# Router logits of 18 tiles summed on VectorE, keys turned once per block, a GpSimd drain per expert unit, and a new order of the first loads

## The chip, the core and the metric

The kernel runs on one core of one Trainium2 chip. The metric is the device time of one execution in microseconds (us), and the time of a version is the median of its runs. The core has TensorE (PE, matmuls; PEld is its weight load), VectorE (DVE), ScalarE (ACT), GpSimd (POOL) and SyncE (SP, which here only issues transfers).

## What is computed

Local attention, a dense MLP and a mixture of experts with one expert per token, one behind the other, over 3072 tokens of 512 features:

```python
# attention: batch 4, heads 8, seq 768, head_dim 64; chunks of 32 queries see
# 8 memory keys, 16 keys to the left, their own 32, and 8 to the right
scores = scale * (q_c @ k_full.T); a = exp(scores - max); a /= sum(a) + 1e-9
out[chunk] = a @ v_full
# MLP, 512 -> 2048 -> 512
h = x @ w_in; g = h * tanh(softplus(h)); y = g @ w_out
# experts: 8, 512 -> 1024 -> 512
xn = y / (norm(y) + 1e-6); en = expert_emb / (norm(expert_emb) + 1e-6)
logits = xn @ en.T / tau; e = argmax(logits); gate = softmax(logits)[e]
out = gate * (relu(y @ w1[e]) @ w2[e])
```

All matmuls that matter are done with operands split into a high and a low float32r part, three products each.

## The kernel before, in words

**The work and its tiles.** 24 attention pairs (128 queries of all heads each) fill 8 blocks of 384 tokens. The MLP goes through 128 units: a unit is one block with one slice of 128 of the 2048 hidden features, 12 matmuls into `p_h` (`mm_h`), the activation on ACT and DVE, 9 matmuls into `p_y` (`mm_y`). Blocks 0 and 1 do their first 8 slices, then block 2 all 16, then blocks 1 and 0 their second 8, then the others. A block yields three tiles of 128 tokens: 24 tiles. Behind the MLP come 16 expert units of one or two slots of 128 gathered tokens.

**What sets the order.** Everything is written down as jobs in a `Plan`: a key, a function, the engines that may do it with a cost, a rank, what it comes after, and which buffers it gets or uses. `Plan.order` picks at each step the job of lowest rank that can start by the planner's own costs and latencies, and by that fixes the order on every engine and on each queue. `NUDGE` is a table of offsets to the ranks. Engines run their queue in order. Until the first `mm_h`, wherever the planner sees PE waiting, it puts in *fills*: matmuls on constants (`p_fill`, L1573) whose result nobody reads.

**Keys, per pair** (`pairs`, L420). Three transposes on PE: the queries (`p_qT`, 128 columns), one key tile of 104 rows (`p_kT`: memory keys and the front of the window) and a second one of 72 rows (`p_k`), with their own loads `load_k1` and `load_k2`; five copies `kT(m)` (L517) spread them into the four windows of 64 keys that the scores use. Neighbouring windows overlap, so some keys are loaded and turned twice.

**Weights of the MLP** (`piece`, L351). 32 pieces of 512 KB, loaded by SP (L360, L363), each then taken apart on DVE with ACT and POOL beside it: sign, bias, high, low, and the parts `hi` and `lo`. The first blocks wait for these pieces.

**Rows of a finished tile** (`rows`, L796). The tile is scaled (`out`), stored to `y_d`, turned on PE (`T`, L832, `p_yT`, 4 transposes), split into three bf16 parts (`b1` a cast on ACT or DVE, `r1` L844, `b2`, `b3` L850) and multiplied with the bf16 parts of the expert embedding in 12 matmuls (`L`, L864, `p_lg`), which DVE adds up (`L2`, L870). The last three tiles (`i >= T1`) take a float32 form instead: a copy and 4 float32 matmuls (L859). ACT squares the row and sums it (`sq`, L853).

**Expert units** (`unit`, L1257). Gathers and scatters of rows are indirect transfers that POOL issues (L1278, L1500); POOL also makes three of the eight low weight parts per unit (L1356). Behind the scatters of units 5, 10 and 14 stands a `drain` of POOL (`RETIRE`, L1593).

## Time and profile before

| | |
|---|---|
| median of 3 runs (lowest, highest) | 1026.44 us (1025.91, 1028.74) |
| the profiled execution, its own time | 1026.37 us |
| span of that execution | 1024.6 us |
| PE busy | 1000.1 us, 98% |
| DVE busy | 756.4 us, 74% |
| ACT busy | 670.8 us, 65% |
| POOL busy | 184.8 us, 18% |
| moved by DMA | 129.06 MB, mean 126 GB/s |
| mean granted TensorE clock | 0.995 |

The span runs from the first to the last instruction that the profile holds, and the execution's own time is 1.8 us longer. "Busy" is the time in which an engine had at least one instruction in work. PE at 98% over the whole says little by itself: matmuls overlap and fills count as busy. What bounds the kernel has to be read stage by stage.

### The profile page before, as it was taken

What the parts mean: (1) busy time and instruction counts of PE and PEld (TensorE: products, weight loads), DVE (VectorE), ACT (ScalarE), POOL (GpSimd) and SP (SyncE); (2) the same over time, 40 slices, a digit from 0 to 9 for tenths busy, and PEclk for the clock granted to TensorE, in tenths of its full rate; (3) what the DMA queues carried; (4) which work ended last, traced back from release to release, by engine and by line L of the source; (5) the groups of instructions that cost most, each with busy time, mean ns of one, the idle gap of its engine ahead of it and who ended that gap; (6) DMA issues with size and microseconds to landing.
All of it is one profiled execution on the core that took longest, in us unless ns stands there. A gap on an engine that the chain in (4) does not pass through costs nothing. (4 is left out here: it accounts for less than half of the span.)

```text
span 1024.6 us, 23081 instructions
## 1 busy us (share of the span) xinstructions
PE 1000.1 (98%) x8875; PEld 886.0 (86%) x8875; DVE 756.4 (74%) x1583; ACT 670.8 (65%) x1577; POOL 184.8 (18%) x130
## 2 busy tenths in 40 slices
PE   7899999999999999999999999999999999899997
PEld 6788898888888888888888888888998988888986
DVE  4999999576776667667667658978959668676862
ACT  5799888677867778778778768665624343443541
POOL 5010100000000000000000000010137565565642
PEclk9999999999999999999999999999999999999999
DMA  9997651032341121122112100088099877468300
GB/s 186 261 251 210 168 151 34 5 121 54 85 102 43 38 71 36 38 55 64 42 43 55 26 1 32 1 271 315 25 305 373 293 227 248 154 207 286 107 32 23
DMA packets 162297, 129.06 MB, mean 126 GB/s; under 512 B 104050, under 2 KB 133346, under 8 KB 161924
## 3 DMA queue, kind: packets, MB, share of 16 engines
q1 hardware_dynamic: 155348, 111.20, 37.7%
q0 software_dynamic: 5104, 15.89, 4.5%
q8 instruction: 72, 1.18, 0.5%
q10 hardware_dynamic: 1728, 0.43, 0.3%
q14 instruction: 45, 0.37, 0.1%
HBM read 119.81 MB, written 16.52 MB: 133 GB/s over the span
## 5 line engine op out<-in xcount | busy, mean ns | idle before, releaser
L726 PE MATMUL p_h<-xt,win_h 128*128 128x384 f32 x1024 | 268.7, 344 | 0.4 <-DVE rn L755 0.3
L726 PEld LDWEIGHTS p_h<-xt,win_h 128*128 128x128 f32 x1024 | 181.5, 189 | 7.3 <-DVE rn L755 0.9
L726 PE MATMUL p_h<-xt,win_l 128*128 128x384 f32 x512 | 172.9, 338 | 0.0
L1356 DVE TENSOR_TENSOR elo<-eraw,ehi 128x1024 fp32r<-128x1024 f32 x89 | 130.1, 1476 | 41.0 <-ACT ehi L329 37.9
L329 ACT CAST ehi<-eraw 128x1024 fp32r<-128x1024 f32 x89 | 92.5, 1049 | 103.0 <-PE p_y L1474 61.9
L772 PE MATMUL p_y<-wout_h,gh 128*128 128x512 f32 x384 | 157.4, 410 | 2.1 <-ACT gh L329 2.1
L772 PE MATMUL p_y<-wout_h,gl 128*128 128x512 f32 x384 | 152.7, 398 | 0.1
L772 PE MATMUL p_y<-wout_l,gh 128*128 128x512 f32 x384 | 152.3, 397 | 0.0
L1474 PE MATMUL p_y<-ehi,hh 128*128 128x512 f32 x432 | 142.3, 398 | 0.0
L1384 PE MATMUL p_h<-xs,ehi 128*128 128x256 f32 x704 | 125.2, 279 | 0.2 <-DVE hh L1401 0.2
L745 DVE SCALAR_TENSOR_TENSOR m<-sq,rn 128x384 f32<-128x384 f32 x128 | 71.2, 556 | 62.5 <-ACT rn L319 61.7
L749 ACT ACTIVATE m<-m,cf 128x384 f32<-128x384 f32 x128 | 79.0, 617 | 51.2 <-DVE m L745 50.1
L1384 PEld LDWEIGHTS p_h<-xs,ehi 128*128 128x128 f32 x704 | 108.8, 188 | 2.1 <-PE p_h L1384 0.4
L1356 POOL TENSOR_TENSOR elo<-eraw,ehi 128x1024 fp32r<-128x1024 f32 x39 | 95.1, 2438 | 80.2 <-ACT ehi L329 45.1
L752 DVE SCALAR_TENSOR_TENSOR rn<-m,rn 128x384 f32<-128x384 f32 x128 | 71.4, 558 | 37.4 <-ACT m L749 36.7
L1384 PE MATMUL p_h<-xs,elo 128*128 128x256 f32 x352 | 98.3, 279 | 0.0
L1474 PEld LDWEIGHTS p_y<-ehi,hh 128*128 128x128 f32 x432 | 81.1, 188 | 18.4
L726 PEld LDWEIGHTS p_h<-xt,win_l 128*128 128x128 f32 x512 | 96.6, 189 | 0.0
L763 DVE TENSOR_TENSOR gl<-rn,gh 128x384 fp32r<-128x384 f32 x128 | 71.1, 556 | 23.6 <-ACT gh L329 19.9
L772 PEld LDWEIGHTS p_y<-wout_h,gl 128*128 128x128 f32 x384 | 72.6, 189 | 17.6 <-DVE gl L763 0.5
L772 PEld LDWEIGHTS p_y<-wout_h,gh 128*128 128x128 f32 x384 | 72.5, 189 | 15.1 <-ACT gh L329 2.3
L1474 PE MATMUL p_y<-elo,hh 128*128 128x512 f32 x216 | 85.3, 395 | 0.0
(272 smaller groups left out, 1761.8 us busy)
## 6 DMA issues: line engine op xcount, KB each, us to landing
eraw<-in_moe_w_dram SPq DMA_DIRECT2D x128, 512.0 KB
vn<-in_v_dram SPq DMA_DIRECT2D x162, 56.0 KB
raw<-in_moe_w_in_dram SPq DMA_DIRECT2D x16, 512.0 KB
raw<-in_moe_w_out_dram SPq DMA_DIRECT2D x16, 512.0 KB
y_d<-ysb SPq DMA_DIRECT2D x24, 256.0 KB
qn<-in_q_dram SPq DMA_DIRECT2D x22, 256.0 KB
kn<-in_k_dram SPq DMA_DIRECT2D x18, 192.0 KB
kn<-in_k_dram SPq DMA_DIRECT2D x17, 128.0 KB
```

What stands on the lines that cost most here:

```text
L329: (nc.scalar.copy if e == A else nc.vector.tensor_copy)(out, src)
L726: nc.tensor.matmul(p, w, xt[j][:, a, kk, :], start=(n == 0), stop=(n == len(ops) - 1))
L745: nc.vector.scalar_tensor_tensor(t, tl["sq", s], 4.0, tl["rn", s], ALU.add, ALU.mult)
L749: nc.scalar.activation(t, t, AF.Square, bias=c15)
L752: nc.vector.scalar_tensor_tensor(tl["rn", s], tl["m", s], 0.75, tl["rn", s], ALU.add, ALU.mult)
L763: engs[e].tensor_sub(t, tl["rn", s], tl["gh", s].bitcast(F32))
L772: nc.tensor.matmul(yp[yh][t], x[:, c], w[g][:, o, :], start=(first and n == 0), stop=(final and n == 2))
L1356: engs[e].tensor_sub(tl["elo", j], raw[b, second, c], tl["ehi", j].bitcast(F32))
L1384: nc.tensor.matmul(p[:, o, :], w[:, kk, s], v[:, kk, :], start=(kk == 0 and m == 0), stop=(kk == KDM - 1 and m == 2))
L1474: nc.tensor.matmul(tl["yy", u][a], v[:, kk, s], w[:, k, :], start=(kk == 0 and m == 0), stop=(kk == KEF - 1 and m == 2))
```

## The change

Five things are changed, and the planner then orders everything anew.

1. **Logits.** For the 18 tiles below `TL` the transpose, the three-way split and the 12 matmuls are gone. The normalised embeddings are stored once to DRAM (`en_d`) and each row is loaded back, spread over the 128 partitions (`load_e`, 48 loads of 256 KB in all); each tile is loaded back from `y_d` (`again`, 18 loads of 256 KB); and DVE multiplies tile and row and sums along the row in one instruction (`one`, `scalar_tensor_tensor` with `accum_out`), 8 per tile, 144 in all. The other six tiles take the float32 form on PE that three had. `sq` overwrites the tile as before.
2. **Keys.** One key tile of 128 rows per pair is loaded and turned (`p_kT`, 128 columns), shifted by 8 against the query block; the 24 keys ahead of it come out of the previous pair's windows by an SBUF copy (`kT0`), and only the first pair of each of the four batches loads and turns a second tile of 32 rows (`p_k`). The windows of all but the first three pairs now lie in one tile that pairs share.
3. **Drains.** One `drain` of POOL per expert unit, ahead of the unit's first scatter and behind the last unit's, and one behind the load of `x_p`: 17 in place of 3.
4. **First loads.** Loads of the first three pairs and of the first six weight pieces may go to SP or to ACT's queue; pieces no longer wait for keys; ranks of pieces go by the unit that needs them.
5. **The planner** gets other constants (latency, bandwidth for short rows, a limit on parts in flight, a smaller gap before tiled matmuls) and a new `NUDGE` table.

The core of the diff (`PLACE` is empty, so `place` changes nothing; `CUT` is (8, 8) and stands for the earlier `HALF`):

```diff
-RETIRE = {5: 4000, 10: 1500, 14: 1500}
+TL = T1 - TPB
-LATENCY, START, SLACK, RING = 2000.0, 1100.0, 34.0, 8
+LATENCY, START, SLACK, RING, PARTS, LANDING, CROWD = 2100.0, 1100.0, 34.0, 8, 1950, 500, 25000
     if b in tiled:
-        return 0 if a in tiled else 150
+        return 0 if a in tiled else 60
 NUDGE = dict(
-    acta0=-0.6, acta1=-1.74, acta2=38.91, acta3=-92.06, actb0=-1.76, actb1=-96.54, actb2=-7.29, actb3=-209.5,
+    acta0=-33.93, acta1=-84.13, acta2=-17.25, acta3=-57.93, actb1=-3.85, actb2=0.92, actb3=-38.42, att01=15.82,
...
 # piece
-        plan.dma(k("load"), load, dict(SP=470), 2 ** 19, r - 4 if n > 3 else 2 * n - 83, [{0: ("issue", "k2", 1), 1: ("issue", "k2", 1), 2: ("issue", "mem", 2)}.get(n, ("issue", "load", n - 1))], [(raw_tag(n), raw)])
+        plan.dma(k("load"), load, {"SP": 470, A: 470} if n < 6 else dict(SP=470), 2 ** 19 * 350 / 262, r - 4 if n > 3 else 2 * n - 83, [("issue", "load", n - 1)] if n else [], [(raw_tag(n), raw)])
 # pairs
         def load_k1(e):
...
-            t = tl["kn", P]
-            if spare or i == 0:
-                dma(e, t[0:NMEM], mem_k[b].rearrange("h p d -> p h d"))
-            get_keys(e, t, NMEM, w, w + K1 - NMEM)
+            get_keys(e, tl["kn", P], 0, w + PREV, w + PREV + 2 * QB)
+        def kT0(e):
+            t = own_kT()
+            if i == 0:
+                p = tl["T", "k2", P]
+                copy(e, t[:, :, 0, 0:K2], p)
...
+            else:
+                o = tl["kT", P - 1]
+                copy(e, t[:, :, 0, NMEM:K2], o[:, :, 3, SEEN - PREV:])
+                if spare:
+                    copy(e, t[:, :, :, 0:NMEM], o[:, :, :, 0:NMEM])
+        def kT1(e):
+            t, p = tl["kT", P], tl["T", "kT", P]
+            copy(e, t[:, :, :, K2:], p.rearrange("p j (c n) -> p j c n", c=4))
+            x = p[:, :, CHUNK - PREV:CHUNK]
+            copy(e, t[:, :, 1:4, NMEM:K2], bass.AP(tensor=x.tensor, offset=x.offset, ap=[x.ap[0], x.ap[1], [CHUNK, 3], x.ap[2]]))
-        job(("Tk", P, 0), turn("kT", "kn", K1), {E: 350}, rank=R(0), after=[("k1", P)], use=[kh], get=[("a", t2), (ktt, kt)])
-        job(("Tk", P, 1), turn("k2", "kn2", K2), {E: 250}, rank=R(0), after=[("k2", P)], use=[k2s], get=[("a", t3)])
+        if start:
+            job(("Tk", P, 1), turn("k2", "kn2", K2), {E: 290}, rank=R(0), after=[("k2", P)] + ([("S", P - 1)] if P > 2 else []), use=[k2s], get=[("a", t3)])
+        job(("Tk", P, 0), turn("kT", "kn", 128), {E: 436}, rank=R(0), after=[("k1", P)] + ([("S", P - 1)] if P > 2 else []), use=[kh], get=[("a", t2)])
 # rows
+        def again(e):
+            nc.sync.dma_start(out=tl["yio", t][:, 1], in_=y_d[half, :])
+        def one(x):
+            def f(e):
+                nc.vector.scalar_tensor_tensor(junk, tl["yio", t][:, 1], 1.0, tl["en", j, x], ALU.mult, ALU.mult, accum_out=lg[:, i, x:x + 1])
+            return f
-        slow = i < T1
...
-            job(k("r1"), r1, {V_: 602}, rank=R[1], after=[k("b1")], use=[p1, yt, yb])
-            job(k("b2"), b2, {A: 520, V_: 335, G: 588}, rank=R[1], after=[k("r1")], use=[yt, yb])
-            job(k("b3"), b3, {G: 1225, V_: 602}, rank=R[1], after=[k("b2")], use=[yt, yb])
-        job(k("L"), L, {E: 315 if slow else 858}, rank=R[1], after=[k("b3" if slow else "b1"), ("em", 4)], get=[("a", p2)], use=[yb if slow else yt])
+        if i >= TL:
...
+            job(k("L"), L, {E: 858}, rank=R[1], after=[k("b1"), ("em", 4)], get=[("a", p2)], use=[yt])
...
+            return
+        plan.dma(("yre", j, t), again, dict(SP=470), 2 ** 18, at_(0) - 3, [k("store")] + ([("ye", before, t, x) for x in range(NE)] if g else []), use=[y])
+        for x in range(NE):
+            if t == 0:
+                def load_e(e, x=x, tag_e=tag_e):
+                    tl["en", j, x] = io.tile([128, DM], F32, tag=tag_e, bufs=1 if tag_e == "eb" else 2, name="en")
+                    nc.sync.dma_start(out=tl["en", j, x], in_=en_d[x:x + 1, :].to_broadcast([128, DM]))
...
+            job(("ye", j, t, x), one(x), {V_: 680}, rank=at_(x), after=[("yre", j, t), ("en", j, x)] + ([pv] if pv else []), use=[y, ("en", j, x)])
 # unit
+            if main and a == 0:
+                job(("retire", u), lambda e: nc.gpsimd.drain(), {G: 700}, rank=base + end + 1.3 * nt, after=[("put", u, a), ("retire", u - 1)] + ([("scatter", u - 1, 0)] if u else []))
 # main
+    job(("retire", -1), lambda e: nc.gpsimd.drain(), {G: 2500}, rank=100, after=[("xload",)])
```

What this does to the order is shown at two places. The first is the head of SP's queue, the start of the program. `qn` and `qkn` are queries (the latter with keys behind them), `kn` and `kn2` keys, `raw` a weight piece, `vn` values. Before:

```order
L1567 DMA cf_63<-in_consts_dram 128x256
L314 DMA qn_113<-in_q_dram 128x8x64
L314 DMA kn2_115<-in_k_dram 72x8x64
L314 DMA qkn_117<-in_q_dram 128x8x64
L314 DMA kn2_154<-in_k_dram 72x8x64
L314 DMA qkn_156<-in_q_dram 128x8x64
L360 DMA raw_163<-in_moe_w_in_dram 128x2x512
L314 DMA qkn_156<-in_mem_k_dram 8x8x64
L314 DMA qkn_156<-in_k_dram 96x8x64
L360 DMA raw_218<-in_moe_w_in_dram 128x2x512
```

And with the change:

```order
L1618 DMA cf_63<-in_consts_dram 128x256
L350 DMA qn_112<-in_q_dram 128x8x64
L350 DMA raw_118<-in_moe_w_in_dram 128x2x512
L350 DMA raw_120<-in_moe_w_in_dram 128x2x512
L350 DMA qkn_130<-in_k_dram 128x8x64
L350 DMA vn_94<-in_v_dram 56x4x64 x4
L350 DMA qkn_227<-in_k_dram 128x8x64
L350 DMA raw_435<-in_moe_w_in_dram 128x2x512
```

The first two weight pieces moved from the seventh and tenth place to the third and fourth; queries and keys of the first pairs now come partly by ACT's queue.

The second place is DVE's queue in the MLP, some 36 units in. `m`, `rn`, `gl` and `gh` are steps of a unit's activation. Before, where a tile of block 2 is split and its logits are added up (`yt`, `yb`, `lg`):

```order
L745 SCALAR_TENSOR_TENSOR m_3402<-sq_3358,rn_3399 128x384
L870 TENSOR_REDUCE lg_66<-p_lg_3404 128x8
L329 CAST yb_3425<-p_yT_3351 128x512
L752 SCALAR_TENSOR_TENSOR rn_3399<-m_3402,rn_3399 128x384
L844 TENSOR_TENSOR yt_3424<-p_yT_3351,yb_3425 128x512
L755 SCALAR_TENSOR_TENSOR rn_3399<-rn_3399,p_h_3288 128x384
L329 CAST gh_3453<-rn_3399 128x384
L850 TENSOR_TENSOR yb_3425<-yt_3424,yb_3425 128x512
```

And with the change, where the tile times an embedding row is summed (`junk,lg<-ysb,en`):

```order
L800 SCALAR_TENSOR_TENSOR rn_3376<-m_3396,rn_3376 128x384
L803 SCALAR_TENSOR_TENSOR rn_3376<-rn_3376,p_h_3332 128x384
L365 CAST gh_3420<-rn_3376 128x384
L893 SCALAR_TENSOR_TENSOR junk_64,lg_66<-ysb_3347,en_2859 128x512
L811 TENSOR_TENSOR gl_3425<-rn_3376,gh_3420 128x384
L893 SCALAR_TENSOR_TENSOR junk_64,lg_66<-ysb_3349,en_2859 128x512
L793 SCALAR_TENSOR_TENSOR m_3442<-sq_3417,rn_3423 128x384
L893 SCALAR_TENSOR_TENSOR junk_64,lg_66<-ysb_3353,en_2859 128x512
```

The split is gone, and sums stand between the steps of a unit's activation. Counted over the whole order, of the 144 sums 50 stand in units 40 to 55 and the rest in units 32 to 39 and 56 to 112. PE's order holds 260 fills in place of 150, all ahead of the first `mm_h`.

## Rows read from the trace of the kernel before

**Rows 1.** Busy time of each engine by stage (busy, number of instructions), TensorE clock, DMA
```profile
core 0: us, PE busy (x) PEld busy (x) DVE busy (x) ACT busy (x) POOL busy (x), PEclk, DMA share, GB/s
0.00:42.10 42.10, 35.03 (x672) 28.65 (x673) 25.98 (x75) 24.39 (x98) 13.91 (x25) 1.00 1.01 220
42.10:133.00 90.90, 84.38 (x1104) 73.72 (x1102) 90.10 (x208) 80.67 (x241) 6.19 (x7) 0.98 0.83 216
133.00:168.60 35.60, 35.60 (x246) 31.83 (x245) 35.49 (x80) 32.19 (x80) 0.00 (x0) 1.00 0.39 97
168.60:676.20 507.60, 507.60 (x4648) 448.55 (x4648) 354.31 (x841) 384.82 (x967) 6.64 (x8) 1.00 0.19 49
676.20:1019.30 343.10, 337.46 (x2213) 303.28 (x2211) 250.48 (x384) 148.09 (x195) 157.11 (x89) 0.99 0.62 210
```

**Rows 2.** What PE waited for: us in total, times, longest us
```profile
PE p_k L506 <- DMA kn<-in_k_dram: 5.6, 3, 2.8
PE p_xT L1320 <- DMA vn<-y_d,gi: 3.1, 2, 2.9
```

**Rows 3.** PE in order of time, 226 to 235 us: start, length, line, instruction, count
```profile
226.11 0.46 PE L864 MATMUL p_lg<-embT,yb 128*128 128x24 bf16 x12
226.43 0.64 PE L832 MATMUL p_yT<-cf,ysb 128*128 128x128 f32 x4
226.90 0.60 PE L506 MATMUL p_qT<-cf,qn 128*128 128x128 f32 x4
227.26 0.48 PE L772 MATMUL p_y<-wout_h,gh 128*128 128x512 f32 x1
...
229.44 0.52 PE L506 MATMUL p_kT<-cf,kn 104*128 104x104 f32 x4
229.74 0.60 PE L726 MATMUL p_h<-xt,win_h 128*128 128x384 f32 x2
...
234.80 0.42 PE L506 MATMUL p_k<-cf,kn 72*128 72x72 f32 x4
235.02 0.60 PE L726 MATMUL p_h<-xt,win_h 128*128 128x384 f32 x2
```

**Rows 4.** The same view at 702 us: one tile's float32 logits
```profile
702.51 0.96 PE L859 MATMUL p_lg<-cf,yt 128*128 128x8 f32 x8
```

**Rows 5.** The same view: the first fills, and a run of them at 26 us
```profile
3.26 1.68 PE L1573 MATMUL p_fill<-cf 128*128 128x256 bf16 x7 [3.26 <-DMA cf<-in_consts_dram]
...
26.49 2.46 PE L1573 MATMUL p_fill<-cf 128*128 128x256 bf16 x21
28.89 0.74 PE L597 MATMUL p_PT<-cf,pr 128*128 128x128 f32 x4
```

**Rows 6.** SP's queue in order of time: the first weight piece
```profile
7.07 0.92 SPq L360 DMA_DIRECT2D raw<-in_moe_w_in_dram  x1
```

**Rows 7.** Groups of DVE: shapes, count, busy us, mean ns, idle before, releaser
```profile
L745 DVE SCALAR_TENSOR_TENSOR m<-sq,rn 128x384 f32<-128x384 f32 x128 | 71.2, 556 | 62.5 <-ACT rn L319 61.7
L755 DVE SCALAR_TENSOR_TENSOR rn<-rn,p_h 128x384 f32<-128x384 f32 x128 | 70.4, 550 | 2.4
L844 DVE TENSOR_TENSOR yt<-p_yT,yb 128x512 f32<-128x512 f32 x21 | 14.4, 687 | 1.2 <-ACT yb L329 0.8
L850 DVE TENSOR_TENSOR yb<-yt,yb 128x512 bf16<-128x512 f32 x21 | 14.4, 685 | 0.3 <-ACT yb L329 0.2
L321 DVE TENSOR_SCALAR raw<-raw 128x512 f32<-128x512 f32 x12 | 5.2, 431 | 0.0
L819 DVE SCALAR_TENSOR_TENSOR ysb<-p_y,ysb 128x512 f32<-128x512 f32 x6 | 4.0, 683 | 0.0
L329 DVE COPY pT<-p_PT 128x512 f32<-128x512 f32 x3 | 2.1, 687 | 0.2
```

**Rows 8.** Groups of ACT: reading out the sum of a squared row
```profile
L853 ACT ACTIVATION_READ_ACCUMULATOR ysb<-ysb 128x1 f32 x24 | 4.6, 190 | 0.0
```

**Rows 9.** Busy time in the stretch of units 40 to 55
```profile
245.00:328.90 83.90, 83.90 (x925) 73.77 (x917) 60.84 (x137) 63.83 (x174) 0.00 (x0) 1.00 0.29 74
```

**Rows 10.** One line's instructions: the drains of POOL (min/median/max ns)
```profile
L1593 POOLq DRAIN  x3: 4423/6629/7557, 848.6 to 1003.3; - x3
```

**Rows 11.** Groups of POOL: low parts of expert weights, columns as in rows 7
```profile
L1356 POOL TENSOR_TENSOR elo<-eraw,ehi 128x1024 fp32r<-128x1024 f32 x39 | 95.1, 2438 | 80.2 <-ACT ehi L329 45.1 <-DVE ehi L329 18.5 <-PE p_y L1474 5.5
```

More of the change, by code (lines that the diff above doesn't have):

```diff
@@ L38 @@
 KEF = EF // 128
-HALF = KFF // 2
-LEAVE = 2
+CUT = (8, 8)
+LEAVE = len(CUT)
 FIRST = 6
@@ L121, in part, with place @@
+BY = dict(A="Activation", D="DVE", G="Pool", S="SP", E="PE")
+def place(key):
+    x = PLACES.get(".".join(str(x) for x in key), "")
+    return float(x.rstrip("ADGSE") or 0), BY.get(x[-1:])
+ATT = dict(q="q", k1="k", k2="l", Tq=1, Tk=1, qT=1, kT=1, v=2, mem="m", mem0="m", S=3, mx=3, ex=4, rg=5, rc=5, norm=5, PT=6, pT=6, V=7, xh=7, xl=7)
 def part(key):
@@ L164, in __init__, with job @@
         self.bufs, self.jobs, self.users, self.getter = bufs, {}, {}, {}
-    def job(self, key, fn, on, rank, after=(), get=(), use=(), lat=130, tiled=False, dmas=0):
+    def job(self, key, fn, on, rank, after=(), get=(), use=(), lat=130, tiled=False, dmas=0, parts=0):
         uses = list(use) + [h for _, h in get]
@@ L194, in order, with landed @@
         self.log = []
-        rings = {"Pool": [], "SP": []}
+        rings, parts = {"Pool": [], "SP": []}, {"Pool": [], "SP": [], "Activation": []}
         rings["Activation"] = rings["SP"]
-        def landed(e, n):
+        def landed(e, n, p):
             ring = rings[e]
-            return max([0.0] + [end.get(ring[x], np.inf) - 400 * i for i in range(n) for x in [len(ring) - RING + i] if 0 <= x < len(ring)])
+            r = max([0.0] + [end.get(ring[x], np.inf) - 400 * i for i in range(n) for x in [len(ring) - RING + i] if 0 <= x < len(ring)])
+            left = PARTS - p
+            for key, m in reversed(parts[e] if e != "Pool" else []):
+                left -= m
+                if left < 0:
+                    return max(r, end.get(key, np.inf) - LANDING - self.jobs[key]["on"]["Q"] * (1 + left / m))
+            return r
         ready = {k: START for k, n in todo.items() if n == 0}
@@ L492, in mem @@
         def mem(e):
-            if spare:
-                tl["vn", P] = wp.tile([128, 2, 2, H // 2, D], F32, tag=vts, name="vn")
             t = tl["vn", P] if spare else vall
@@ L905, in attn_moe_moe_kernel @@
+        job(k("L2"), lambda e: None, {"none": 0}, rank=at_(NE - 1), after=[("ye", j, t, x) for x in range(NE)])
     gi, si = const.tile([128, NSLOT], I32, name="gi"), const.tile([128, NSLOT], I32, name="si")
@@ L1580, in attn_moe_moe_kernel @@
         mlp(s)
-    for i in range(NTILE):
+    for i in done:
         rows(i)
```

260 lines of the change are left out of this document (135 added, 125 removed).

## The prediction

> **What bounds the kernel now.** I read the busy times by stage first, then what PE waited for, then PE in order of time where the change touches it, and last the groups of DVE and POOL.
>
> The stages [rows 1] tell five different stories. In the first 42.1 us PE is busy 35.0, fills included, so 7.1 are idle, and 3.26 of these lie before the constants land [rows 5]. From 42.1 to 133.0 DVE is the bound: 90.10 of 90.90 us, with 6.5 us in which PE has nothing. The third stage, 133.0 to 168.6, has PE at 35.60 of 35.60 beside DVE at 35.49: PE can be full beside a full DVE. The fourth, 168.6 to 676.2, is the long one: PE 100%, DVE 354.3 of 507.6 (70%), ACT 384.8. Any PE time taken off there is gained one for one as long as DVE keeps up. In the last, PE is busy 337.5 of 343.1, and POOL 157.1, so it has 186 us to spare. PE's named waits are few: 5.6 us for keys, the longest 2.8, and 3.1 for gathered rows [rows 2].
>
> So: stage 4 gains what leaves PE, stages 1 to 3 gain what leaves DVE or arrives earlier, and stage 5 is hardly touched.
>
> **Stage 4, PE.** A tile's 12 bf16 matmuls take from 226.11 to the next start at 226.43, .32 us, and its 4 transposes from 226.43 to 226.90, .47: together .79 [rows 3]. Starts, not lengths, count, since matmuls overlap. 18 tiles lose both: 18 x .79 = 14.2 us off. Three more tiles get float32 logits: 8 matmuls of two tiles take .96 [rows 4], .48 per tile against .32; with the extra copy that they share I take .5 more a tile, +1.5.
>
> Keys: a pair loses its `p_k`, .22 (234.80 to 235.02), and widens `p_kT` from 104 columns, .30, to 128, which the queries' transpose prices at .36 (226.90 to 227.26) [rows 3]. That is .16 off per pair. 13 of the 24 pairs lie in stage 4: 2.1 off, less two batch starts that keep a small second transpose, at most .22 each: 1.7 off. PE's share of stage 4: -14.2 + 1.5 - 1.7 = -14.4, to 493 us.
>
> **Stage 4, DVE.** This is what the gain costs. A sum reads two 128x512 float32 tiles. The trace has no such instruction with an accumulated output. The nearest row below is L819, 128x512 with a PSUM operand, 683 ns; that two operands in SBUF cost hardly more than one beside PSUM is seen in L745, 556 ns, against L755, 550, both of 384 columns [rows 7]. An upper price adds what ACT pays to read out such a sum, 190 ns [rows 8]: 873. I take 683, as the row nearest in shape and engine. 144 x .683 = 98.4 us added. Off goes the split, r1 and b3, 21 x (.687 + .685) = 28.8 [rows 7]. DVE has 354.3 + 98.4 - 28.8 = 423.9 of 493, 86%; at the upper price 451, 92%. Over the stage it fits. That the averages hide a crowd has to be asked: 50 of the 144 sums stand in units 40 to 55, a stretch of 83.9 us with DVE at 60.84 [rows 9]. There 50 x .683 = 34.2 come in and five tiles' splits (6.9) go: 88.1 us of DVE, against 83.9 less some 4 for PE. The excess is 8; instructions queued back to back overlap at their ends, and units around it take some, so I take +2.5, between 0 and +10 (the upper price, with 9.5 more, minus what the neighbours take).
>
> The loads for it, 66 x 256 KB = 17 MB, fall into a stage whose DMA share is .19 [rows 1]: nothing by bandwidth; at the upper end see the third rival.
>
> **Stages 1 to 3.** 110 more fills stand ahead of the first `mm_h`. 21 fills take 2.40 us (26.49 to 28.89), .114 each [rows 5]: +12.6 us of PE. But fills are put where PE would wait, so they take the place of waits: stage 1 had 7.1 idle, less the 3.26 ahead of the constants, 3.8. And a PE that starts `mm_h` later finds more weights ready: of the 6.5 idle in stage 2 I take 4.0 off (from 0 to 6.5). The 11 other pairs' keys save 11 x .16 = 1.8 less two small transposes, 1.4. Sum: 12.6 - 3.8 - 4.0 - 1.4 = +3.4, with the bounds +.9 and +11.2.
>
> DVE, the bound of stage 2, gives a second reading of this. Up to unit 16 the changed order gives it six more bias steps (.431), four more pT copies (.687) and nine smaller ones (.431 or less), at most 9.2 us, against three steps fewer (some 1.5) [rows 7]: about +7. Against that, the first weight piece is issued at 7.07 behind six loads [rows 6], now behind two; by sixths that is up to 4.7 us earlier, an estimate. +2.3 by this, +3.4 by PE: they agree well enough to keep the latter.
>
> **Stage 5.** 14 drains more, 13 of them among the expert units. A drain row reads 4.4 to 7.6 us [rows 10], but this contains what POOL still had in work, one low part being 2.44 [rows 11]. POOL's 186 spare us hide them; without that cover each could hold a low part for about 2 us. I take 0, between -3.1 (the wait for gathered rows goes) and +5.
>
> **Sum.** +3.4 - 14.4 + 2.5 + 0 = -8.5. The profiled execution took 1026.37, .07 below the median of the runs, so 1026.4 - 8.5 = **1017.9 us**. The forecast's own bounds: with the low ends (+.9, 0, -3.1) 1009.8; with the high ends (+11.2, +10, +5) 1038, which need not meet; 1009 to 1028 I call its own range.
>
> **The rivals.** *The start gives it back.* The fills are real PE work ahead of `mm_h`, and DVE, busy 90.10 of 90.90, sets stage 2 whatever PE finds ready; then the waits stay and stages 1 to 3 cost +11.2 instead of +3.4: 1025.7, no change that can be told. For it: DVE as the bound. Against: earlier weight pieces.
>
> *The sum takes two passes.* From L745 to L819 an instruction grows by 127 ns for 128 columns, .99 ns a column [rows 7]. If keeping a running sum costs that a second time, 512 columns add .507 and a sum takes 1.19 us. DVE then gets 144 x 1.19 = 171 us, 497 in all for 493, and in units 40 to 55 60.84 + 50 x 1.19 - 6.9 = 113 us stand against 80 of PE [rows 9]. Of these 33 over, the slack of the units around takes a few; 28 stay in place of 2.5: 1043, slower. L745 against L755 shows no such step without a sum. [...]
>
> *SP holds up keys.* 48 rows and 18 tiles are now loaded over SP, each waiting for a buffer that a DVE sum frees, and the queries, keys and values of the pairs in stage 4 stand behind them in the same queue. If DVE falls behind the order by more than a load's lead, a late key load costs PE what rows 2 show, up to 2.8 us. Ten pairs at 2 us: +20, 1038, slower than before. It decides where DVE has no slack, in units 40 to 55 [rows 9]. Against it: over the stage DVE has 14% left.
>
> *Drains hold the low parts.* A drain ahead of a unit's first scatter stops POOL until its work is done, and low parts for the next unit queue behind it; 13 units at 2 us of PE: +26, 1044. Against it: 186 us of idle POOL [rows 1].
>
> **How the numbers follow.** The forecast gets .62, the start .15, SP .12, the drains .06, two passes .05. About .3% of the time, 3.1 us, is what a measurement can tell from no change: faster is below 1023.3, slower above 1029.5. Of the forecast's .62, .58 lies below 1023.3, and the start adds .06 (its bounds reach there when the wait shrinks a little), the low end of SP .02: faster .66. The start's other .07, .03 of the forecast and .03 of SP's: same .13. The rest, .21, slower. The range leaves out 2 in 10: from 1007 (a stage 2 that gains more) to 1034, which takes in the start and the beginning of SP's case and leaves slow ends out.
>
> **What would show it.** Right: stage 4, from the start of unit 24 to the experts, some 12 us shorter; PE idle in it near 0; the sums' group at about 683 ns; DVE near 86% there; the first `mm_h` at 46 to 49 us instead of 42.1 and no 6.5 us idle behind it; stage 5 at 343. Wrong: sums at 870 or 1190 ns, PE idle in units 40 to 55 released by DVE's activation steps; waits of PE for `kn`, `qn` or `vn` loads of several us, issued late by SP; PE waiting for `elo` behind a drain; stage 2 ending as late as the fills are long. A stage 4 that is as long as before would refute the main term.

## The result, and the profile after

The changed kernel takes 1038.72 us (median of 6 runs, 1033.34 to 1042.67) against 1026.88 of the kernel before, run beside it: a ratio of 1.0115 (95% interval 1.0092 to 1.0138). It is **slower by 1.15%**; the forecast was 1017.9 us, faster.

The profiled execution of the change is the shortest of the six, 1033.34 us. A second profile of the same kernel (the last experiment) was of one of 1043.19. Both are used, so that what they share can be told from what varies. First the busy times by stage of the first profile, cut at the same events as [rows 1]: first `mm_h`, end of stage 2, unit 24, the experts (in both kernels the first `mm_h` of the last MLP unit), the end; the last line is units 40 to 55, for [rows 9].

```profile
core 0: us, PE busy (x) PEld busy (x) DVE busy (x) ACT busy (x) POOL busy (x), PEclk, DMA share, GB/s
0.00:59.30 59.30, 47.76 (x759) 39.57 (x759) 35.84 (x88) 21.54 (x83) 13.61 (x25) 0.94 0.83 202
59.30:150.70 91.40, 88.37 (x1096) 77.26 (x1095) 88.78 (x216) 73.00 (x221) 6.15 (x7) 0.94 0.69 182
150.70:185.50 34.80, 34.68 (x174) 30.40 (x173) 34.64 (x81) 28.80 (x59) 0.00 (x0) 1.00 0.23 67
185.50:678.70 493.20, 492.49 (x4367) 436.81 (x4365) 397.85 (x1042) 365.81 (x935) 6.62 (x9) 1.00 0.31 83
678.70:1031.50 352.80, 338.65 (x2219) 304.29 (x2216) 269.66 (x395) 145.45 (x188) 162.59 (x92) 0.99 0.61 207
259.00:341.80 82.80, 82.47 (x908) 72.05 (x905) 78.03 (x212) 63.55 (x187) 2.05 (x3) 1.00 0.57 151
```

The same by differences, the last stage taken to the end of the span (348.4 us before):

| us against before | forecast | first profile | second profile |
|---|---|---|---|
| stages 1 to 3 (unit 24 starts at 168.6 before) | +3.4 | +16.9 | +17.4 |
| stage 4 | -11.9 | -14.4 | -14.5 |
| last stage | 0 | +4.4 | +13.9 |
| together | -8.5 | +6.9 | +16.8 |

The gain is there and a little larger than forecast. It is lost at the start, the same in both executions, and at the end, where the two differ by 9.5 us. How far single executions scatter can be told from the experiments below, since some leave the order up to unit 24 as it was: six executions with the order of before start unit 24 at 168.6 to 175.0 us (mean 172.2), four with that of the change at 185.5 to 189.3 (mean 187.1). So the start costs some 15 us on the mean, and 16.9 is counted from the earliest of the six.

**The sums.** Groups of DVE and, for the last line, of low parts of expert weights; columns as in [rows 7].

```profile
L893 DVE SCALAR_TENSOR_TENSOR junk<-ysb,en 128x512 f32<-128x512 f32 x144 | 99.0, 687 | 4.0 <-DMA ysb<-y_d 3.6
L893 DVE DVE_READ_ACCUMULATOR junk<-ysb,en 128x1 f32 x144 | 11.8, 82 | 0.0
L1409 DVE TENSOR_TENSOR elo<-eraw,ehi 128x1024 fp32r<-128x1024 f32 x89 | 141.8, 1603 | 30.4 <-ACT ehi L365 29.2
```

By these rows a sum is 687 ns and reading out the accumulator 82. In order of time (start, length) the read-out costs nothing more:

```profile
240.17 0.69 DVE L893 SCALAR_TENSOR_TENSOR junk<-ysb,en 128x512 f32<-128x512 f32 x1
240.78 0.08 DVE L893 DVE_READ_ACCUMULATOR junk<-ysb,en 128x1 f32 x1
240.78 0.55 DVE L811 TENSOR_TENSOR gl<-rn,gh 128x384 fp32r<-128x384 f32 x1
```

It starts before the sum's row ends, and the next step starts with it: .61 us from the sum's start to the next step's (the median of the 144 too), where a step of 128x512 without a sum took .60 before (from 630.87 to 631.47 us). Units 40 to 55 take 82.8 us with DVE busy 78.0, against 83.9 and 60.84 [rows 9]: the crowd fits.

**The start.** ACT's queue in order of time (start, length; ACTq is the issue of a transfer):

```profile
7.74 0.36 ACTq L350 DMA_DIRECT2D raw<-in_moe_w_out_dram  x1
8.14 0.45 ACTq L350 DMA_DIRECT2D qkn<-in_q_dram  x1
...
28.77 5.29 ACTq L350 DMA_DIRECT2D vn<-in_v_dram  x4
34.11 0.62 ACT L365 CAST wout_h<-sp 128x512 fp32r<-128x512 f32 x1 [7.54 <-DMA vn<-in_v_dram]
34.63 0.31 ACT L615 ACTIVATE pr<-p_S,pr 128x64 f32<-128x64 f32 x1
```

And PE, the transposes of the queries of pairs 1 and 2, and the first `mm_h`, with DVE's first step on a weight piece:

```profile
7.74 0.43 DVE L405 TENSOR_SCALAR sp<-raw 128x512 int32<-128x512 int32 x1 [6.87 <-DMA raw<-in_moe_w_in_dram]
...
18.61 0.63 PE L539 MATMUL p_qT<-cf,qkn 128*128 128x128 f32 x4 [2.42 <-DMA qkn<-in_q_dram]
...
29.99 0.63 PE L539 MATMUL p_qT<-cf,qkn 128*128 128x128 f32 x4 [1.42 <-DMA qkn<-in_q_dram]
...
59.27 0.60 PE L774 MATMUL p_h<-xt,win_h 128*128 128x384 f32 x2
```

Before, the issue of these queries, their transposes and DVE's first step on a weight piece stood at:

```profile
2.31 0.42 SPq L314 DMA_DIRECT2D qkn<-in_q_dram  x1
...
10.40 0.60 PE L506 MATMUL p_qT<-cf,qkn 128*128 128x128 f32 x4
...
17.06 0.42 DVE L369 TENSOR_SCALAR sp<-raw 128x512 int32<-128x512 int32 x1
```

So queries that were issued at 2.31 us and turned at 10.40 are now issued at 8.14, behind a 512 KB weight piece, and turned at 18.61. Later, issuing four value loads keeps ACT from its exponentials for 5.29 us. DVE starts on weights sooner (7.74 us instead of 17.06), and it gains nothing: until unit 24 it is busy 159.3 us and idle 26.2, before 151.6 and 17.0. So of the 16.9 us, 7.7 are more DVE work and 9.2 are more DVE idle time. Almost none of it comes back behind the first `mm_h`: from there to unit 24 it takes 126.2 us, before 126.5, though PE now idles only 3.0 us in stage 2 instead of 6.5. PE's mean granted clock was also lower than before, 0.94 in stages 1 and 2 against 1.00 and 0.98; the run without fills, below, tells whether that matters.

**The end.** SP's waits for the routing (`ei`), and its issue of the expert weights, us from the start; then ACT's waits for these weights (total, times, longest):

```profile
SPq L1344 <- POOL ei L1217: 94.5, 2, 56.3
...
678.42 31.50 SPq L1356 DMA_DIRECT2D eraw<-in_moe_w_dram  x24
...
ACT ehi L365 <- DMA eraw<-in_moe_w_dram: 10.3, 6, 3.7
```

Before, the same three read:

```profile
SPq L1291 <- POOL ei L1165: 86.3, 2, 47.0
...
671.46 31.98 SPq L1303 DMA_DIRECT2D eraw<-in_moe_w_dram  x24
...
ACT ehi L329 <- DMA eraw<-in_moe_w_dram: 5.6, 3, 3.4
```

The weights are issued 7 us later, and the routing's last logits come later too. Before, and then with the change:

```profile
634.27 0.18 DVE L870 TENSOR_REDUCE lg<-p_lg 128x8 f32<-128x24 f32 x1 [0.47 <-PE p_lg L864]
```

```profile
641.10 0.17 DVE L905 COPY lg<-p_lg 128x8 f32<-128x8 f32 x1 [0.59 <-PE p_lg L902]
```

They are ready 6.8 us later, while the experts start only 2.5 later (678.7 against 676.2). So PE enters the last stage with less in hand.

### The profile page after: what moved, and what is told of

Read it like the earlier page. It is cut to its first block, busy times and chain, and to the rows that moved or that the text cites. A ratio compares the mean times of both kernels' runs of the same rounds, so it can differ in the third digit from the quotient of the medians.

```text
span 1031.5 us, 22836 instructions
## 1 busy us (share of the span) xinstructions
PE 1001.9 (97%) x8605; PEld 888.3 (86%) x8605; DVE 826.8 (80%) x1819; ACT 634.6 (62%) x1481; POOL 189.0 (18%) x133
## 3 DMA queue, kind: packets, MB, share of 16 engines
q8 instruction: 70, 1.15, 0.5%
## 4 chain that ended last, share of the span: by engine, by line
PE 62%; DMA 10%; DVE 10%; issue 8%; POOL 5%; ACT 2%; SPq 2%; POOLq 1%; ACTq 0%; DVEq 0%
PE p_h L774 22%; PE p_y L820 21%; PE p_y L1527 4%; PE p_h L1437 4%; POOL elo L1409 4%; DMA eraw<-in_moe_w_dram 3%; PE p_X L654 2%; DMA vn<-y_d,gi 2%; DMA out_dram<-yo,si 2%; PE p_S L592 2%; PE p_h L1471 1%; DMA qn<-in_q_dram 1%; SPq L1356 1%; PE p_fill L1624 1%; POOLq L1561 1%
## 5 line engine op out<-in xcount | busy, mean ns | idle before, releaser
L774 PEld LDWEIGHTS p_h<-xt,win_h 128*128 128x128 f32 x1024 | 184.8, 190 | 10.6 <-DVE rn L803 2.9
L1409 DVE TENSOR_TENSOR elo<-eraw,ehi 128x1024 fp32r<-128x1024 f32 x89 | 141.8, 1603 | 30.4 <-ACT ehi L365 29.2
L1437 PE MATMUL p_h<-xs,ehi 128*128 128x256 f32 x704 | 128.6, 284 | 3.0 <-DVE rn L803 1.8
L1409 POOL TENSOR_TENSOR elo<-eraw,ehi 128x1024 fp32r<-128x1024 f32 x39 | 98.6, 2529 | 37.7 <-ACT ehi L365 23.2
L893 DVE SCALAR_TENSOR_TENSOR junk<-ysb,en 128x512 f32<-128x512 f32 x144 | 99.0, 687 | 4.0 <-DMA ysb<-y_d 3.6
L778 ACT ACTIVATE sq<-p_h 128x384 f32<-128x384 f32 x128 | 63.0, 493 | 57.0 <-PE p_h L774 52.7
L820 PEld LDWEIGHTS p_y<-wout_h,gl 128*128 128x128 f32 x384 | 72.2, 188 | 17.4
```

The lines of the kernel that those rows point to most:

```text
L774: nc.tensor.matmul(p, w, xt[j][:, a, kk, :], start=(n == 0), stop=(n == len(ops) - 1))
L778: nc.scalar.activation(t, tl["h", s], AF.Tanh, scale=0.5)
L820: nc.tensor.matmul(yp[yh][t], x[:, c], w[g][:, o, :], start=(first and n == 0), stop=(final and n == 2))
L893: nc.vector.scalar_tensor_tensor(junk, tl["yio", t][:, 1], 1.0, tl["en", j, x], ALU.mult, ALU.mult, accum_out=lg[:, i, x:x + 1])
L1409: engs[e].tensor_sub(tl["elo", j], raw[b, second, c], tl["ehi", j].bitcast(F32))
L1437: nc.tensor.matmul(p[:, o, :], w[:, kk, s], v[:, kk, :], start=(kk == 0 and m == 0), stop=(kk == KDM - 1 and m == 2))
```

## The experiments

My theory was that the start alone decided: three changes there (fills, order of the loads, which engine does which step) delay the first `mm_h`, and DVE carries the delay on. Rivals were that the sums cost more around them than in their row, that the keys or the drains do, and that the start's order is a bar of latency that no single edit moves. Each ratio below is against the kernel before in the same set of runs.

### One part at a time

**Sums alone** on the kernel before (part 1 of the change with its six float32 tiles, nothing else), and a second profiled execution of it:

```diff
+TL = T1 - TPB
-    embT = const.tile([128, KDM, 3 * NE], BF16, name="embT")
+    junk = const.tile([128, DM], F32, name="junk")
...
+        plan.dma(("yre", j, t), again, ...)
+            job(("ye", j, t, x), one(x), {V_: 680}, rank=at_(x), ...)
```

> The kernel before with the sums alone: 18 tiles' logits on DVE as in the change, loads of rows and tiles with them; keys, drains, first loads, planner constants and NUDGE stay as before, and 150 fills as before. Theory 'the sums are a gain, the start loses it': unit 24 starts at 167 to 171 as before, stage 4 falls from 507.6 by 14.2 less some 2 for three more float32 tiles, to 495, total 1014 (1010 to 1019). Rival 'DVE gives it back' (without the tuned offsets the sums crowd in units 40 to 55): stage 4 above 503, total 1022 or more, with PE waiting there for the activation on DVE.

> The kernel before with the sums alone once more, for a second profiled execution: the first took 1023.5, the lowest of ten (median 1026.9), with stage 4 at 499.8 and unit 24 at 172.2. Theory 'start': the difference to the first lies in the start of unit 24, stage 4 is within 1.5 us of 499.8. Rival 'sums vary' (their loads land late in some executions): stage 4 is 502 or more.

Measured: 1026.89 against 1025.23, 1.001 (0.9991 to 1.0029), and 1030.4 in the second profiled execution. The order up to unit 24 is that of before, and stage 4 takes 499.8 us (501.1 in the second) instead of 507.6. I had expected 495 and a total of 1014. So the sums bring 7.8 of stage 4, and the total does not show them: unit 24 started 3.6 and 6.1 us later in these two executions with an unchanged order, a spread that the start has by itself. Units 40 to 55 of the sums alone, and PE's longest wait in stage 4:

```profile
248.50:333.50 85.00, 83.10 (x918) 72.78 (x916) 78.79 (x214) 65.98 (x194) 4.82 (x7) 1.00 0.56 147
...
PE p_h L730 <- DVE rn L759: 2.9, 3, 1.4
```

PE idles 1.9 us there and 3.5 in the whole stage, most of it released by a DVE step of the activation: here the crowd is to be seen, at a small price.

**Sums that yield** (two sets of runs):

```diff
-        at_ = lambda x: 33 + (NE * TPB * g + TPB * x + t) * 80 / (NE * TL)
+        at_ = lambda x: 60 + (NE * TPB * g + TPB * x + t) * 70 / (NE * TL)
```

> The run of before with the sums alone (stage 4 499.8, 85.0 us in units 40 to 55 with 1.9 of them without PE), with the ranks of the sums 27 units later, so that a step of a unit's activation goes ahead of a sum whenever both are ready. Theory 'crowding by rank': PE idle in stage 4 falls from 3.5 to under 1 us, stage 4 to 497 or less, total 2 to 3 us less than with the sums alone, 1023 to 1025. Rival 'there is no room' (in units 40 to 55 DVE has 41 sums and its own work, whatever the rank): stage 4 stays at 499 to 501 and the total at 1026 to 1029.

> The kernel before with the sums alone and their ranks 27 units later, once more, for a second interval and a second profiled execution. If the first result (ratio .9953, .9937 to .997) holds: 3 to 6 us faster than before, stage 4 at 498 to 500, last stage 346 to 349. If it was the luck of one chip: within 2 us of before.

Measured: 1022.18 against 1026.76, 0.9953 (0.9937 to 0.997); again, in 12 runs, 1022.71 against 1025.74, 0.9966 (0.9947 to 0.9984). Units 40 to 55 of it:

```profile
251.90:336.30 84.40, 84.29 (x986) 74.13 (x985) 78.91 (x218) 65.88 (x196) 5.08 (x7) 1.00 0.60 159
```

The same DVE work, and in these units PE's idle time is gone (84.29 of 84.40). Over the whole stage it is not: PE idles 2.9 us instead of 3.5, and stage 4 takes 498.9 us (498.5 the second time) instead of 499.8, where I had expected under 1 and at most 497. The version is faster than the kernel before by .3 to .5%, and faster than the change and the sums alone; but fewer crowded units explain only a part of that, and where the rest comes from is not shown.

**No sums** in the changed kernel; all 24 tiles go through the float32 form:

```diff
-TL = T1 - TPB
+TL = 0
```

> The changed kernel with TL = 0: all 24 tiles take the float32 logits on TensorE, no sums, no embedding rows and no tiles loaded back. The main term of the prediction (a tile off PE is worth its PE time, and DVE has room for the sums): stage 4 grows from 493.2 by 18 tiles x .95 us = 17.1, to 510, total 1056. Rival (the sums cost a part of it back through DVE or SP's queue): stage 4 grows by less than 12, total under 1051; if the spread of the changed kernel (1033 to 1043) comes from the 66 loads of the sums, it shrinks to that of before (3 us).

Measured: 1081.62, 1.0563 (1.0523 to 1.0603); stage 4 529.1 us, +35.9, of which 27.7 are PE's work (520.2 us against 492.5, 1.54 a tile) and 8.2 its idle time (8.9 against .7). Unit 24 is later too (190.7) and the last stage longer (357.9). This weighs the sums against the float32 form; against the bf16 form that the change replaces, .79 a tile, only the run with the sums alone weighs them.

**Keys alone** on the kernel before (part 2 as in the change; the first pieces wait for the one key load that is left):

```diff
-... [{0: ("issue", "k2", 1), 1: ("issue", "k2", 1), 2: ("issue", "mem", 2)}.get(...)], ...
+... [{0: ("issue", "k1", 1), 1: ("issue", "k1", 1), 2: ("issue", "mem", 2)}.get(...)], ...
```

> The kernel before with the new keys alone (one turned tile per pair, the overlap copied from the previous pair's windows, the second transpose at batch starts), the first loads on the queues they had, the weight pieces behind the second pair's keys as before. 166 fills. Theory 'start loads': the keys are not what made the start late; unit 24 starts at 166 to 171, stage 4 loses 1 to 2 us, total 1021 to 1027. Rival 'the key chain' (a pair's windows now wait for the previous pair's, so the first three pairs run one behind the other): the first mm_h at 48 or later and unit 24 at 175 or later, total 1031 or more.

Measured: 1047.17, 1.0199 (1.0165 to 1.0232). Stage 4 falls by 4.4 us to 503.2; some 2 of them are one pair's transposes and scores that now stand ahead of unit 24 (48 `p_qT` in the stage instead of 52). The first `mm_h` starts at 48.6 and unit 24 at 196.9, with DVE busy 162.3 and idle 34.6 until then. These are the signs of the rival, the key chain; but `NUDGE` was written for other jobs and the whole start was planned anew, so the price of the keys themselves isn't measured by this, and it isn't excluded either.

**Drains alone** on the kernel before (part 3), and **the changed kernel with the old three drains**; then the changed kernel in its own order with the 14 others left out:

```diff
+            if main and a == 0:
+                job(("retire", u), lambda e: nc.gpsimd.drain(), {G: 700}, ...)
...
+RETIRE = {5: 4000, 10: 1500, 14: 1500}
...
+        thin = [("retire", u) for u in range(-1, 16) if u not in (5, 10, 14)]
+        order = [x for x in order if x[0] not in thin]
```

> The kernel before with a drain of GpSimd ahead of each expert unit's first scatter and one behind the load of x_p, in place of three. Theory 'hidden' (POOL has 186 us to spare): total 1026 within 2 us, the last stage 348 as before. Rival 'drains hold the low parts': TensorE waits for elo behind drains, the last stage 4 us or more longer, total 1030 or more.

> The changed kernel with the three drains of before in place of its 17. Theory 'hidden': the last stage stays at 352 to 354 as in the changed kernel (its extra waits come from elsewhere), total 1034 to 1042. Rival 'drains hold the low parts': the last stage goes back to 348, total 4 us less.

> The changed kernel in its own order with 14 of its 17 drains left out (those of units 5, 10 and 14 stay). Theory 'drains' (on the kernel before they cost 3.7 us, 1.6 to 5.6): the last stage falls from 353 to 362 to about 349, DVE's busy time in it from 270 to 251 as in the run with three drains, total 1034 to 1036. Rival 'not the drains': the last stage stays at 353 or more and the total at 1037 to 1041.

Measured: 1029.32, 1.0036 (1.0016 to 1.0055); 1035.45, 1.0099 (1.0065 to 1.0132); 1041.66, 1.0161 (1.0137 to 1.0184). Added to before they cost 3.7 us (1.6 to 5.6) of the total, though in the profiled execution the last stage is as long as before (348.8 us against 348.4), so where they cost it is not seen. Taken from the change they give back nothing that can be told: the last stage still takes 357.7 and 357.6 us.

### The start

**Keys first**, and with it **the old places of the loads** (queries and pieces by SP alone, keys of two pairs by ACT, their values by POOL), both ordered anew:

```diff
-... [("issue", "load", n - 1)] if n else [], ...
+... [{0: ("issue", "k1", 1), 1: ("issue", "k1", 1), 2: ("issue", "mem", 2)}.get(n, ("issue", "load", n - 1))], ...
...
-        both = ("SP", A) if first else ("SP",)
+        both = (A,) if P < 2 else ("SP",)
-            plan.dma(("v", P, h), load_v(h), on={G: 700 * n, "SP": 430 * n, A: 430 * n} if first else dict(SP=400 * n), ...
+            plan.dma(("v", P, h), load_v(h), on={G: 700 * n} if P < 2 else dict(SP=400 * n), ...
```

> The changed kernel, with one thing undone: the first three weight pieces are issued behind the keys of the second pair (pieces 0 and 1) and behind the memory values of the third (piece 2), as before; SP and ACT may still both issue first loads. The planner then puts 151 fills ahead of the first mm_h, where the changed kernel has 260. Theory 'order' (weight pieces ahead of queries make the queries of pairs 1 and 2 land 10 to 14 us after their issue, and the attention of block 0 is late): the first mm_h starts at 45 to 49 us instead of 59.3, unit 24 at some 173 instead of 185.5, total 1026 (1022 to 1030). Theory 'ACT's queue' (loads issued by ACT hold its exponentials and copies): ACT still issues a dozen loads, so the first mm_h stays at 55 or later and the total at 1034 or more. Theory 'fills' (each fill is PE work): 109 fills fewer at .114 us, first mm_h at about 47, total 1026.

> As the run with keys first, and besides the loads of the first pairs and pieces go where they went before: queries and pieces by SP, keys of the first two pairs by ACT, values of the first two by GpSimd. 239 fills stand ahead of the first mm_h, nearly as many as in the changed kernel. Theory 'order': first mm_h at 45 to 49 us, the ACT part adds nothing, total as with keys first, 1026. Theory 'ACT's queue': only now the start recovers, 1024 to 1028, against 1034 or more with keys first. Theory 'fills': 21 fills fewer give 2.4 us, first mm_h at 57, total 1036.

Measured: 1048.2, 1.0246 (1.0211 to 1.028), and 1032.37, 1.0091 (1.0056 to 1.0126). Keys first brought the first `mm_h` to 42.4 us, earlier than I had said, but stage 2 grew to 102.3 with DVE busy 101.3 of them, and unit 24 started at 179.6. An early `mm_h` alone buys little; the weights' steps on DVE stand behind it. That the total missed by 22 us is not the start's doing: against the change the new order also loses 12 us in stage 4 (505.2) and 7 in the last stage (359.9). Units 40 to 55 of it:

```profile
252.00:349.90 97.90, 90.96 (x981) 78.66 (x977) 89.44 (x250) 65.42 (x188) 0.82 (x1) 0.93 0.54 144
```

They take 97.9 us instead of 82.8, hold 57 sums instead of 48, PE idles 6.9 beside a DVE that is busy 89.44, and its clock was granted at 0.93 on the mean: in this order the crowd costs about the +10 that was the forecast's upper end.

**Steps pinned to ACT**, on the last one, ordered anew:

```diff
+    if key[0] == "pT" and key[1] < 8 or key[0] == "gh" and key[1] < 16 or key[0] == "bias" and key[1] < 28:
+        return 0.0, "Activation"
```

> The old-start run's kernel (first mm_h 49.3, unit 24 at 180.0, DVE busy 156.1 and idle 23.9 of it), with three kinds of step pinned to ACT in the start: the copies of pT of the first eight pairs, the bias step of the first 28 weight pieces, the cast to gh of the first 16 units. That takes 3 copies at .687, 7 bias steps at .431 and 6 casts at .35 off DVE, 7.2 us. Theory 'DVE work' (until unit 24 the time is DVE's work plus its idle time, and the change's order gives DVE more work there): DVE busy about 149, unit 24 at 173 to 175, total 1025 to 1028. Rival 'latency' (the start waits for loads and for the attention chain, DVE's work is not what counts): what DVE loses in work it gains in idle time, unit 24 at 178 or later, total 1031 or more.

Measured: 1051.26, 1.0233 (1.0202 to 1.0264). DVE's work until unit 24 fell to 151.7 us, its idle time rose to 30.3, and unit 24 started at 182.0 instead of 180.0. Most of the 19 us by which this run is slower than the last one stand behind that: stage 4 takes 506.5 us against 497.1, the last stage 360.2 against 352.3.

**No fills**, in the changed kernel's order:

```diff
-    plan.fill = lambda e: nc.tensor.matmul(p_fill, fill[:, 0:128], fill[:, 0:256], start=True, stop=True)
+    plan.fill = lambda e: None
```

> The changed kernel without its fills; their result is read by nobody and the rest of the order is the same. Theory 'fills': first mm_h at 47 us or sooner, total 1026 or lower. Theories 'order' and 'ACT's queue': the fills stand in time that PE waits anyway, the first mm_h stays at 58 to 60, and what changes is only the granted clock of the start, total 1037 to 1044.

Measured: 1042.36 (1034.62 to 1052.01), 1.0205 (1.015 to 1.026). The first two stages, columns as above:

```profile
0.00:58.30 58.30, 24.78 (x499) 18.68 (x499) 35.01 (x86) 20.41 (x77) 13.67 (x25) 1.00 0.82 198
58.30:150.30 92.00, 87.39 (x1094) 75.71 (x1095) 89.57 (x218) 73.67 (x225) 6.16 (x7) 1.00 0.70 184
```

First `mm_h` 58.3, unit 24 at 185.2: without one fill the start is as long. The fills are not what delays it, and neither is the clock, which was granted in full (1.00) in both stages here. What then ends last is seen in the chain of waits of this run (start, length, what):

```profile
20.55 13.21 DMA qn<-in_q_dram
...
38.24 0.60 DVE sp L413
38.92 0.66 DVE sp L417
...
40.25 0.69 DVE win_l L435
40.96 0.69 DVE pT L365
```

A late load and then one DVE step behind another.

The next four keep the changed kernel's own order on every engine and move single entries. **Queries early** (right behind pair 0's on SP), **ACT free of loads** behind its first keys (this and the former), **steps to ACT** (all of it), and **ACT free with the drains thinned** (without the steps):

```diff
+        early = [("issue", "q", 1), ("issue", "q", 2)]
+        off = {("issue", "load", 2): "SP", ("issue", "load", 3): "SP", ("issue", "load", 4): "SP", ("issue", "v", 2, 0): "Pool"}
+            return k and e == "DVE" and (k[0] == "pT" and k[1] < 8 or k[0] == "bias" and k[1] < 28 or k[0] == "gh" and k[1] < 16)
```

> The changed kernel in its own order, nothing planned anew; only the query loads of the second and third pair move from ACT's queue, where they stand behind weight pieces, to SP's, right behind the first pair's queries. Theory 'late queries' (in the changed kernel the second pair's queries are issued at 8.14 and land 10.3 us later, the third's are used at 30.0, and the attention of the first block and all that follows waits for them): first mm_h at 50 to 53 instead of 59.3, unit 24 at 176 to 180 instead of 185.5, total 6 to 9 us less than the changed kernel. Rival 'DVE work' (until unit 24 DVE has 7.7 us more to do): first mm_h earlier, but unit 24 stays at 183 or later, since DVE is full from then on.

> As the run with early queries, and the other loads that ACT issues behind its first keys go elsewhere in the same place of the order: three weight pieces to SP, the values of the third pair to GpSimd. Theory 'ACT's queue' (the value loads stood on ACT from 28.8 to 34.1, and the exponentials and casts behind them waited; 3.4 us of DVE's idle time is put down to ACT there): first mm_h 3 us or more earlier than with the early queries alone, unit 24 at 173 to 177. Rival 'ACT was waiting anyway': within 1 us of the run with early queries.

> As the run with ACT free (first mm_h 52.8, unit 24 at 180.1, until then DVE busy 159.3 and idle 20.8), in the same order, with steps that DVE does in the start done by ACT at the same place: 4 copies of pT at .687, 15 bias steps at .431 and 6 casts to gh at .35, 11.3 us less for DVE until unit 24. ACT was busy only 23.1 of the first 52.8 us. Theory 'DVE work' (what is left of the late start is work that the change's order puts on DVE): DVE busy about 148, unit 24 at 168 to 173, total 8 to 11 us less than with ACT free, 1022 to 1027. Rival 'latency': DVE's idle time grows by what it loses in work, unit 24 at 178 or later.

> Early queries, ACT free and thin drains together, in the changed kernel's own order. If the parts add up: unit 24 at 173 to 177, stage 4 at 493, the last stage 349 to 352, total 1018 to 1026, at or below before. If DVE's work holds the start: total 1030 or more.

| | first `mm_h` | unit 24 | DVE busy, idle until it | last stage | ratio (95%) |
|---|---|---|---|---|---|
| queries early | 55.9 | 184.9 | 158.8, 26.2 | 360.5 | 1.0202 (1.015, 1.0255) |
| ACT free | 52.8 | 180.1 | 159.3, 20.8 | 353.4 | 1.0097 (1.0068, 1.0126) |
| steps to ACT | 54.7 | 185.5 | 151.0, 34.5 | 361.1 | 1.0142 (1.0109, 1.0176) |
| ACT free, drains thin | 54.1 | 181.8 | 159.0, 22.8 | 361.9 | 1.0122 (1.006, 1.0184) |

ACT's queue is a cause, of some 5 us at unit 24: without these loads in it the unit starts at 180.1 and 181.8 in two executions, against 184.9 with the queries alone early and 185.5 to 189.3 in the four with the change's order. In the total it does not show: 1.0097 and 1.0122 stand beside the change's 1.0115. The queries, late as they are, are worth .6 us by themselves. What is left is not PE's or DVE's length alone. The chain of waits of "ACT free" runs through fills:

```profile
14.26 10.17 DMA raw<-in_moe_w_out_dram
...
28.01 4.70 PE p_fill L1631 x43
...
35.02 5.67 PE p_fill L1631 x51
```

and with steps moved to ACT, DVE loses 8.3 us of work and gains 13.7 of idle time. Beside 10.5 us for the first weight piece, which it waits for in "ACT free" too (10.6, where the change has 6.9), it now waits for ACT's own steps (total, times, longest; 1.2 us in "ACT free"):

```profile
DVE sp L423 <- ACT raw L365: 6.4, 9, 1.9
```

So the rival held: loads, DVE's steps and fills are bars side by side, and taking one away shows the next. Some 10 of the 15 us stay without a proven single cause. All three taken away at once, in an order made for it, was not run. Nor was the change's start with the old keys, and the keys stay a candidate: every version here that has the new keys starts unit 24 at 179.6 us or later, every one that has the old ones at 175.0 or earlier.

**The changed kernel again**, for the spread of its runs.

> The changed kernel once more, for a second profiled execution: the first took 1033.3, the lowest of six, while the others lie up to 1042.7 with the same order of instructions. Theory 'start' (the loads of the first 60 us land at other times from run to run): whatever this execution differs by shows in the start of unit 24 (185.5 in the first), and stage 4 is within 1.5 us of 493.2. Rival 'expert weights': it shows in the last stage (352.8).

Measured: 1043.19. I had placed the spread in the start; it is in the last stage (362.3 us against 352.8). PE's waits there, second profile and then first:

```profile
PE p_xT L1373 <- DMA vn<-y_d,gi: 7.4, 4, 3.6
PE p_yT L881 <- ACT ysb L355: 3.1, 1, 3.1
PE p_h L1437 <- ACT xs L365: 2.4, 1, 2.4
```

```profile
PE p_yT L881 <- ACT ysb L355: 3.1, 1, 3.1
PE p_xT L1373 <- DMA vn<-y_d,gi: 2.8, 3, 1.1
PE p_h L1437 <- DVE rn L803: 1.8, 1, 1.8
PE p_h L1437 <- DVE hh L1454: 1.0, 1, 1.0
```

Of the 9.5 us the gathers of rows make 4.6; steps on `xs` make 2.2 more; the rest I did not follow. Why the gathers vary stays open. In twelve executions of the change and of versions made from it that keep the sums, the last stage took 352.3 to 362.3 us; in six of the kernel before and of versions that only add sums or drains to it, 346.7 to 352.4. So +4.4 is at the low end of what the change costs there.

## Why the prediction was wrong

**Stage 4: right, with luck in the digits.** Forecast -14.4 of PE and +2.5 for the crowd; measured -14.4 in all. The price of a sum, 683 ns, was near its row (687), and a read-out of the accumulator, the upper price's reason, is there at 82 ns but takes no time of its own. DVE ended at 397.9 us of 493 (81%), not 423.9: the `lg` adds and the `yb` casts of a tile and several `qT` copies left it too, and instructions back to back overlap (the rows of its instructions add up to 453.4 us against 386.1 before, 67 more, its busy time to 43.5 more). The crowd cost nothing that shows in the change, 1.9 us with the sums alone, and some 12 in the order of the run with keys first: that term hangs on the order. The parts are less sure than their sum: the sums alone brought 7.8 (8.7 when they yield) where I had 10.2 with the crowd, and PE's busy time fell by 11.3 where I had 12.7; the keys alone brought 4.4 where I had 1.7, some 2 of it work that had only moved out of the stage. In the change, too, the cut at unit 24 shifts work: the 9 `mm_y` of one unit fall ahead of it and not behind it, some 2 us off, and the scores of one more pair and the transposes of one or two behind it, some 2 us on; that they cancel was not foreseen. One row was misread: 8 float32 matmuls in .96 us [rows 4] are one tile, not two (168 of them for 21 tiles without sums). By starts, which is how the other rows were read, such a tile takes .81 us (702.51 to 703.32) against .32, so +1.5 for three comes out all the same, by luck.

**The sum in two passes: excluded.** 687 ns is about what L819 took with one PSUM operand and no sum, 683 [rows 7], where this rival had estimated 1.19 us. Each of the 144 sums has a read-out of 82 ns on the mean behind it, and by the starts it adds nothing: .61 us from a sum's start to the next step's, .60 before for a step of 128x512 without a sum.

**Stages 1 to 3: the step that failed.** I wrote "12.6 - 3.8 - 4.0 - 1.4 = +3.4", fills taking the place of waits; measured +16.9, some 15 on the mean. The sum was made on PE, and the fills were its price; without any fill the start is as long. The second reading, on DVE, had the work right (about +7; measured +7.7) and its sign wrong for the rest: I took 4.7 off for earlier weight pieces. DVE did begin on them 9.3 us earlier, but its idle time rose by 9.2 instead of falling. I looked at the queue that the pieces left, SP's, and put the loads that entered ACT's queue at nothing: taking them out of it is worth some 5 us (DVE's idle time 20.8 instead of 26.2). That the two readings "agree well" was no evidence: both left out the same thing. The cause of the other 10 us or so stays open; fills and clock are excluded, the keys that pairs now take from one another are not.

**The start gives it back: right in kind, too small.** DVE carried the delay to unit 24 unchanged, 126.2 against 126.5 us, as this rival has it. Its +11.2 had the fills as the cause, and they are not.

**The last stage: wrong.** "I take 0, between -3.1 and +5": measured +4.4, inside these bounds, and +13.9, outside. The wait whose end I put at the low bound, for gathered rows [rows 2], stayed (2.8 us, then 7.4). What I had not seen is that the experts' first waits hang on the routing, which must end earlier with stage 4; it came 6.8 us later, and the waits by which PE enters the stage rose from 2.1 us to 5.9 (the 3.1, 1.8 and 1.0 in the last rows above). Before, the one of them was:

```profile
PE p_y L772 <- ACT gh L329: 2.1, 1, 2.1
```

That the late routing makes these waits is argued from the times; no run moves the routing alone. The drains, +3.7 on the kernel before, show nothing in the changed one when they are taken out, and PE waits .5 us for `elo` at most.

**SP holds up keys: did not happen.** In stage 4 PE idles .7 us.

## What to carry to other kernels

Moving sums from a full engine to one with slack paid here, in that engine's stage, nearly what its rows say (11.3 us of PE's work for 12.7), less what the crowd took back; and how much that is was set by the order, from nothing to some 12 us. When loads change queues, price them on the queue that they enter: what stands ahead of them there, and which of that engine's own steps then stand behind (here ACT's, behind 5.29 us of issuing four value loads). And a planner that orders everything anew hides what an edit does: in two experiments on the start most of the loss came from stages that the edit did not touch. Holding the order and moving single entries keeps that out. Last, one profile is one execution: unit 24 moved by 6 us with an unchanged order.
